# One written-out order replaced by another: a retention layer and a channel mix on one core

## The chip, the core and the metric

The kernel runs on one core of a Trainium2 chip. Five engines work on it side by side, each with an instruction queue that it takes in order: TensorE (PE; its weight loads are PEld), VectorE (DVE), ScalarE (ACT), GpSimd (POOL) and SyncE (SP). The metric is the device time of one execution in microseconds (us). Beside it the profile of one execution gives the span, from its first to its last instruction.

## What is computed

Inputs are q, k and v (4 sequences, 8 heads, 768 tokens, 64 numbers) and the weights of a channel mix. First comes a recurrence over the tokens, per sequence and head, then the mix over the 512 joined numbers of a token:

```python
state = gamma * state + outer(k[t], v[t]);  x[t] = scale * q[t] @ state
xk = mu_k * x + (1 - mu_k) * x_prev;        xr = mu_r * x + (1 - mu_r) * x_prev
h = maximum(xk @ w_k, 0);                   out = sigmoid(xr @ w_r) * (h * h @ w_v)
```

`x_prev` is x one token earlier. `w_k` is 512x1024, `w_v` 1024x512, `w_r` 512x512.

## The kernel before, in words

**Blocks.** The 4x768 tokens are cut into 12 blocks of 256 tokens, numbered 0 to 11, three to a sequence. The recurrence is done a block at a time in matrix form: scores inside the block, a carried state, and the two added up. Blocks 3 and 4, 6 and 7, 9 and 10 share their mix inputs and key matmuls; the others are done alone.

**Pieces and their order.** No scheduler orders the work. The string `ORDER` (from line 24) holds 637 words, and a loop at the end of the kernel goes through it and issues one piece for each. A word is a code, numbers (block first), after `@` the PSUM banks (there are 8, called 0 to 7), and after `~` the engine: v VectorE, a ScalarE, p GpSimd, s SyncE. A word without `~` is TensorE's. The words of one engine, read from left to right, are that engine's queue. So a word's place sets what it stands behind, and its bank sets which earlier result must have been read before it may start.

**The codes**, with the lines under which the profile books them:

- Loads `lq`, `lk`, `lv` (L230, L235) of q, k, v of a block, `wk`, `wr`, `wv` (L735, L738, L742) of weights. From block 2 on, `lk` and `lv` are two DMAs each. The tiles of q, k and v are rings of four.
- TensorE, small tiles: `Tq`, `Tk` transposes (L272, L278); `S` scores (L318, L331, L339); `C` the block's own state (L366, L384, L395); `I`, `J` what the carried state gives (L441); `Y` what the block itself gives (L462, L478, L489).
- TensorE, full 128x128 tiles: `K` the keys xk @ w_k (L572 for the paired blocks, four matmuls of 512 columns; L582 for the others, eight of 256); `R` the gate xr @ w_r (L612, four of 512); `V` the values (L624; a word is four matmuls of 512, so a row block of 128 tokens takes the words V.n.t.0 and V.n.t.1); `Vc` the last row block cut in two halves of columns (L642, eight of 256).
- ScalarE: `Eq`, `Ek` copy the transposes out of PSUM (L241); `t` weights x for block 0 (L542); `Qa` the relu (L591), `Qb` the square (L599, L603), `s` the sigmoid (L618).
- VectorE: `vs` scales v by its decay (L253); `M` masks the scores (L347, L354); `U` adds the carried state (L419); `D` writes x out of PSUM (L507, L514); `dx` the token difference (L529); `X.n.w.j` one quarter j of a block's mix input, w = 0 for xk and 1 for xr (L552 for block 0, else L558); `O` sigmoid times value (L630), `Oc` for the halves (L649). Some `vs`, `U` and `G` words are given to another engine.
- `G` decays the carried state: four instructions on ScalarE (L424), or one on VectorE (L428).
- SyncE: `st` stores a row block of `O` (L637), 128 tokens by 512; `sc` stores a half (L657).
- `z` are matmuls of zeros before and between the first pieces (L703, L710).

**Rings.** A tile is written again only when its readers are done. The results of `O` lie in a ring of four, so `O.n.t` needs the store of block n-2, same t, to have landed. The sigmoids lie in a ring of four as well, the relu outputs too, and `vs` in a ring of three.

The loop that turns words into instructions sets the banks like this:

```python
for word in ORDER.split():
    word, _, at = word.partition("@")
    word, _, eng = word.partition("~")
...
        BANK[key] = [int(x) for x in at]
    CODES[code](ENG.get(eng), *args)
```

Of the kernel before, what the change touches and what calls it, by code (L numbers as in the profile page):

```python
# [29 lines left out]
t.0.0.3~a t.0.0.2~a t.0.0.1~a lv.2~p z.2@4 S.1.1@23 M.1.1~v C.1@01 U.1.0~v z.2@4 I.1@23 S.1.0@67  # L30
X.0.0.1~v t.0.1.2~a X.0.0.2~v Tk.2@0 t.0.1.3~a t.0.0.0~a M.1.0~v X.0.0.0~v z.2@4 Y.1 t.0.1.1~a
X.0.0.3~v Ek.2~a K.0.0@0 K.0.1@6 lq.4~p U.1.1~v G.1~a wr~p lk.4~p D.1~v dx.1~v X.1.0.2~v X.1.0.0~v
K.0.2@1 Qa.0.0~a Qb.0.0~a Qa.0.2~a lq.3~p X.1.0.1~v X.1.0.3~v X.1.1.0~v Qa.0.1~a K.0.3@0 Qa.0.3~a
# [2 lines left out]
Qb.0.2~a Tq.4@01 Eq.4~a Y.2 Qa.1.3~a Qb.1.1~a X.0.1.3~v X.1.1.3~v R.1.1@4 Tk.4@01 Ek.4~a J.2 R.1.0@6
Qa.1.2~a s.1.0~a X.0.1.2~v X.0.1.1~v X.0.1.0~v R.0.1@5 s.0.1~a s.1.1~a R.0.0@7 s.0.0~a S.4.1@01
Qb.1.0~a D.2~v dx.2~v X.2.0.2~v X.2.0.0~v S.4.0@23 Tq.3@4 Eq.3~a X.2.0.1~v wv.1~p X.2.0.3~v Tk.3@7
lq.5~p Ek.3~a K.2.2@5 Qa.2.2~a K.2.3@4 M.4.1~v M.4.0~v Qa.2.3~a Qb.2.3~a lk.6~p S.3.1@67 M.3.1~v
# [7 lines left out]
lq.7~p K.3.7@6 Qa.3.3~a Qa.3.7~a lv.6~p lq.8~p vs.6~v M.5.1~v V.2.0.1 st.0.1~s I.5@67 O.2.0~v
st.2.0~s C.6@23 U.6.0~a U.6.1~v U.6.2~v K.3.6@1 Qa.3.6~a lk.9~p X.3.1.3~v Y.5 Tq.7@45 Eq.7~a U.6.3~v
X.3.1.2~v I.6@01 J.5 X.3.1.0~v D.5~v X.3.1.1~v Qb.3.3~a G.6~a V.2.1.0@2 K.3.1@3 V.2.1.1 O.2.1~v
Qb.3.7~a Qa.3.1~a Qb.3.1~a dx.5~v K.3.4@4 K.3.5@5 Qa.3.5~a X.5.0.0~v X.5.0.3~v R.3.1@2 s.3.1~a  # L50
lv.7~p Qa.3.4~a X.5.0.1~v Qb.3.4~a R.3.0@5 R.4.0@2 s.3.0~a s.4.0~a Qb.3.0~a X.5.0.2~v vs.7~v K.5.2@4
S.7@67 st.1.1~s M.7~v Qb.3.5~a Y.6 Qb.3.6~a lv.10~p C.7@23 U.7.0~v X.5.1.1~v Qa.5.2~a K.5.0@5
R.4.1@6 Qa.5.0~a D.6~v s.4.1~a V.4.0.0@4 V.4.0.1 V.3.1.0@5 U.7.1~v Qb.5.0~a X.5.1.3~v U.7.2~v I.7@01
X.5.1.2~v U.7.3~v Tq.8@67 Eq.8~a X.5.1.0~v O.4.0~v lv.8~p vs.8~v Qb.5.2~a lq.10~p lk.8~p Tk.8@23
Ek.8~a V.3.1.1 V.3.0.0@4 C.8@67 O.3.1~v st.2.1~s st.3.1~s Y.7 dx.6~v D.7~v Tq.10@23 V.3.0.1 Eq.10~a
G.7~a dx.7~v X.6.0.2~v V.4.1.0@5 R.5.1@2 s.5.1~a K.5.3@0 Qa.5.3~a R.5.0@2 U.8.0~v O.3.0~v V.4.1.1
lv.9~p lk.10~p lq.9~p Tk.10@01 s.5.0~a U.8.1~v X.6.0.1~v Ek.10~a X.6.0.0~v Tk.9@23 Ek.9~a K.5.1@7
Qa.5.1~a X.6.0.3~v K.6.0@4 lq.11~p Qb.5.1~a Qa.6.0~a U.8.2~v I.8@01 vs.9~v S.8@23 M.8~v O.4.1~v
st.4.1~s K.6.4@7 Qa.6.4~a vs.10~v X.6.1.2~v K.6.2@6 C.9@23 Qa.6.2~a Qb.6.2~a U.9.0~a Y.8 U.9.1~v
D.8~v U.9.2~v U.9.3~v X.6.1.3~v Qb.5.3~a Tq.9@45 V.5.1.0@6 V.5.1.1 O.5.1~v Eq.9~a lk.11~p K.6.3@7  # L60
Qa.6.3~a K.6.7@4 Qa.6.7~a V.5.0.0@7 C.10@45 Qb.6.0~a X.6.1.0~v S.9@23 M.9~v G.9~a Qb.6.3~a Tq.11@01
Eq.11~a V.5.0.1 dx.8~v X.6.1.1~v st.4.0~s K.6.1@6 Qb.6.7~a Qa.6.1~a Qb.6.1~a X.8.0.3~v X.8.0.0~v
U.10.0~v U.10.1~v K.6.5@2 Qa.6.5~a st.3.0~s lv.11~s K.6.6@0 Qa.6.6~a Qb.6.6~a R.6.0@6 s.6.0~a
O.5.0~v U.10.2~v U.10.3~v R.7.0@2 s.7.0~a R.6.1@7 s.6.1~a I.9@45 X.8.0.2~v S.10@23 Tk.11@01 Ek.11~a
# [6 lines left out]
Qa.9.2~a Qb.9.2~a X.11.0.3~v K.9.5@7 K.9.3@3 K.9.0@2 Qa.9.0~a Qb.9.6~a V.8.0.0@0 V.8.0.1 Qb.9.0~a
Qa.9.5~a Qb.9.5~a Qa.9.3~a O.7.1~v st.7.1~s X.9.1.2~v X.11.0.1~v O.6.0~v K.9.7@1 R.8.1@7 s.8.1~a
K.9.1@5 R.8.0@7 X.9.1.3~v X.11.0.2~v st.6.1~s O.8.1~v R.9.1@4 R.9.0@6 K.11.0@3 K.11.3@2 s.8.0~a
Qa.9.1~a Qb.9.1~a Qb.9.3~a V.10.0.0@5 V.9.0.0@7 Qa.11.0~a Qb.11.0~a Qa.11.3~a s.9.0~a K.9.4@6
R.10.0@2 Qa.9.7~a X.11.1.3~v st.6.0~s K.11.1@1 Qa.11.1~a Qa.9.4~a K.11.2@3 Qb.9.7~a Qb.9.4~a
Qa.11.2~a X.11.1.2~v O.8.0~v st.7.0~s st.8.1~s st.8.0~s V.9.1.0@1 V.10.1.0@6 s.10.0~a V.9.1.1
# [723 lines left out]
```

## Time and profile before

| | before |
|---|---|
| time, median of 3 runs | 153.07 us (153.02 to 153.23) |
| time of the profiled execution | 153.06 us |
| its span | 151.3 us |
| busy: PE, DVE, ACT, POOL | 143.5, 127.5, 103.4, 55.3 us |
| mean granted TensorE clock | 1.000 |
| DMA: bytes, of which GpSimd's queue | 22.16 MB, 14.42 MB |

The profile's page gives the busy time of each engine, the same in 40 slices of the span, and groups of instructions with the mean length of one. Other views list the instructions of one engine in order of time, count busy time in chosen stretches, and tell for the instructions of one line how long they took and how long their DMAs took to land. A row of the timeline names start, length, engine, line, operation and count; in brackets stands the idle time ahead of it and what ended it. Lengths of neighbours overlap a little, because an engine starts the next instruction before the last one has drained; what a queue advances by is the distance of starts.

### The profile page before, as it was taken

The numbers are of one execution on the slowest core, as the hardware profiler recorded it, in microseconds if no ns is written. First come the engines' busy times: TensorE is split into PE (matmuls) and PEld (weight loads), VectorE is DVE, ScalarE is ACT, GpSimd is POOL, SyncE is SP. The second block draws the span as 40 slices with busy tenths as digits, with TensorE's granted clock in tenths as the row PEclk, the third lists the DMA queues.
The fourth block names the chain that finished last, engine by engine and source line by source line (L and its number), as shares of the span: only waits on it lengthen the run. The fifth ranks groups of instructions, "written<-read, shape, count | busy, mean of one in ns | idle before, by whom it ended". The sixth has DMA issues, their size and how long they took to land.

```text
span 151.3 us, 5540 instructions
## 1 busy us (share of the span) xinstructions
PE 143.5 (95%) x2426; PEld 82.9 (55%) x2426; DVE 127.5 (84%) x212; ACT 103.4 (68%) x195; POOL 55.3 (37%) x65
## 2 busy tenths in 40 slices
PE   7878799999999999999999999999999999999991
...
PEclk9999999999999999999999999999999999999999
DMA  5999999999999999999999019311000005500433
GB/s 126 235 230 194 208 228 195 167 247 215 196 166 203 233 260 119 269 289 197 230 172 122 6 45 281 100 41 39 0 4 0 4 0 215 201 0 0 153 129 139
DMA packets 45624, 22.16 MB, mean 146 GB/s; under 512 B 37400, under 2 KB 41248, under 8 KB 45600
## 3 DMA queue, kind: packets, MB, share of 16 engines
q0 software_dynamic: 38704, 14.42, 74.5%
...
q8 instruction: 19, 0.31, 0.8%
q10 hardware_dynamic: 304, 0.18, 0.6%
...
## 4 chain that ended last, share of the span: by engine, by line
PE 86%; ACT 3%; DVE 3%; POOL 2%; DMA 2%; issue 1%; SPq 0%; DVEq 0%
PE ps L624 27%; PE ps L612 14%; PE ps L572 14%; PE ps L582 13%; PE ps L278 3%; PE ps L441 2%; DMA k2s<-in_k_dram 2%; PE ps L272 2%; DVE a L354 2%; PE ps L478 1%; ACT qT L241 1%; POOL vs L253 1%; PE ps L366 1%; PE ps L462 1%; PE ps L642 1%; POOL k L230 1%
## 5 line engine op out<-in xcount | busy, mean ns | idle before, releaser
L624 PE MATMUL ps<-wv,k2s 128*128 128x512 f16 x184 | 44.1, 380 | 0.0
L591 ACT ACTIVATE kr<-ps 128x512 f32<-128x512 f32 x48 | 27.8, 593 | 12.6 <-PE ps L582 6.6
L624 PEld LDWEIGHTS <-k2s 128*128 128x128 f16 x184 | 17.1, 98 | 18.9 <-ACT k2s L603 0.4
L630 DVE SCALAR_TENSOR_TENSOR os<-ps,rs 128x512 f32<-128x512 f32 x23 | 15.7, 684 | 11.9 <-ACT rs L618 9.4
L612 PE MATMUL ps<-wr,xr 128*128 128x512 f16 x96 | 23.5, 379 | 0.0
L582 PE MATMUL ps<-xk,wk 128*128 128x256 f16 x192 | 23.2, 273 | 0.0
L572 PE MATMUL ps<-xk,wk 128*128 128x512 f16 x96 | 23.0, 379 | 0.0
L618 ACT ACTIVATE rs<-ps 128x512 f32<-128x512 f32 x24 | 13.6, 597 | 12.9 <-PE ps L612 12.1
L230 POOL DMA_DIRECT2D k<-in_k_dram x20 | 17.7, 902 | 10.1 <-PE ps L384 6.8
L582 PEld LDWEIGHTS <-wk 128*128 128x128 f16 x192 | 18.1, 98 | 3.7
L241 ACT COPY qT<-ps 128x1024 f16<-128x1024 f16 (+1 forms) x13 | 12.3, 946 | 9.2 <-PE ps L278 7.8
L558 DVE SCALAR_TENSOR_TENSOR xr<-dx,mu,xT 128x256 f16<-128x256 f32 (+1 forms) x32 | 17.9, 577 | 0.1
L230 POOL DMA_DIRECT2D v<-in_v_dram x18 | 16.0, 911 | 3.9 <-DVE a L354 2.2
L558 DVE SCALAR_TENSOR_TENSOR xk<-dx,mu,xT 128x256 f16<-128x256 f32 (+1 forms) x32 | 17.0, 579 | 0.2
L354 DVE TENSOR_TENSOR a<-ps,c_sb 128x1024 f16<-128x1024 f32 (+1 forms) x14 | 14.6, 1066 | 0.7 <-PE ps L339 0.4
L603 ACT ACTIVATE k2s<-kr 128x512 f16<-128x512 f32 x24 | 14.8, 631 | 0.3
L612 PEld LDWEIGHTS <-xr 128*128 128x128 f16 x96 | 9.1, 98 | 10.7 <-issue 0.5
L572 PEld LDWEIGHTS <-wk 128*128 128x128 f16 x96 | 9.1, 98 | 10.5
L599 ACT ACTIVATE k2s<-kr 128x512 f16<-128x512 f32 x24 | 14.5, 627 | 0.3
L529 DVE TENSOR_TENSOR dx<-xT 128x1024 f32<-128x1024 f32 x11 | 13.4, 1222 | 0.2
L241 ACT COPY kT<-ps 128x1024 f16<-128x1024 f16 (+1 forms) x13 | 12.2, 944 | 1.9 <-PE ps L272 1.4
L253 DVE TENSOR_TENSOR vs<-v,csm_sb 128x1024 f16<-128x1024 f32 x10 | 12.2, 1217 | 0.0
...
## 6 DMA issues: line engine op xcount, KB each, us to landing
...
```

The source lines that it names most:

```text
L230: e.dma_start(out=dst[:, :, i * D : i * D + D], in_=src[:, i * P : i * P + P].rearrange("h p d -> p h d"),)
L241: e.copy(out=out, in_=in_)
L354: nc.vector.tensor_tensor(out=a_full(n)[:, i, :, j0:j1], in0=pairs(banks("S", n, i, j0))[:, :, j0:j1], in1=(below if wide(n) else causal[: ...
L558: nc.vector.scalar_tensor_tensor(out=XM[w](k)[:, j, t0:t1], in0=DX(k)[:, j, t0:t1], scalar=mu[:, w * NCO + j : w * NCO + j + 1], in1=x[:, ...
L572: nc.tensor.matmul(banks("K", n, g), lhsT=wk16[:, co, g * P : g * P + P], rhs=XM[0](k)[:, co, :], start=(co == 0), stop=(co == NCO - 1),)
L582: nc.tensor.matmul(pz[:, i, :], lhsT=wk16[:, co, fo * P : fo * P + P], rhs=XM[0](k)[:, co, m * TM + t0 : m * TM + t1], start=(i == 0 and c ...
L591: nc.scalar.activation(out=kr, in_=banks("K", n, g, *u), func=AF.Relu)
L599: nc.scalar.activation(out=k2s[:, n % 3 : n % 3 + 2, g, :], in_=kr, func=AF.Square,)
L603: nc.scalar.activation(out=K2(n)[:, w * g : w * g + w, t0:t1], in_=kr.rearrange("p a t -> p (a t)").rearrange("p (i t) -> p i t", i=w), fu ...
L612: nc.tensor.matmul(banks("R", n, tb), lhsT=XM[1](k)[:, co, t : t + P], rhs=wr16[:, co, :], start=(co == 0), stop=(co == NCO - 1),)
L624: nc.tensor.matmul(banks("V", n, tb), lhsT=K2(n)[:, fo, tb * P : tb * P + P], rhs=wv16[:, fo, :], start=(fo == 0), stop=(fo == NFO - 1),)
L630: nc.vector.scalar_tensor_tensor(out=OS(2 * n + tb), in0=banks("V", n, tb), scalar=1.0 / (KSC * KSC), in1=RS(2 * n + tb), op0=ALU.mult, op ...
```

## The change

All words from the scores of block 1 on are put in another order; the 59 words ahead of them stay. Both orders hold the same 637 words when engine and bank are left aside. Beside the order, 118 words get other banks, and three words another engine: `vs.3` goes from GpSimd to VectorE, `G.9` and `G.10` from ScalarE to VectorE. Functions, tile shapes, rings and transfers are the same. Of the diff, which replaces 51 lines of `ORDER` by 51, the lines that the text below speaks of:

```diff
-lk.3~p vs.2~v Tq.2@1 X.1.1.2~v K.1.3@6 K.1.0@0 C.2@7 U.2.0~v lv.3~p Eq.2~a S.2.1@23 M.2.1~v S.2.0@45
-M.2.0~v Qb.0.3~a lv.4~p K.1.1@1 X.1.1.1~v Qa.1.0~a t.0.1.0~a K.1.2@7 I.2@23 Qb.0.1~a Qa.1.1~a wv.0~p
...
-S.3.0@01 vs.3~p C.3@23 U.3.0~a Qb.2.2~a K.2.1@4 Qa.2.1~a K.2.0@2 Qa.2.0~a I.3@45 lq.6~p vs.4~v
-C.4@67 U.3.1~v X.2.1.1~v V.0.1.0@3 M.3.0~v V.1.0.0@2 G.3~a U.4.0~v I.4@01 X.2.1.3~v U.4.1~v J.3
...
-O.1.0~v Tq.6@01 Eq.6~a Tk.6@45 Ek.6~a st.0.0~s lk.7~p st.1.0~s V.1.1.0@3 V.1.1.1 O.1.1~v s.2.0~a
...
-dx.10~v X.9.0.3~v X.9.0.0~v Y.11 Qb.8.0~a X.9.0.2~v R.7.1@6 s.7.1~a X.9.0.1~v V.7.0.0@7 V.7.0.1
...
-V.10.0.1 s.9.1~a O.9.1~v st.9.1~s Qb.11.2~a Qb.11.3~a O.10.0~v st.10.0~s R.10.1@4 V.9.0.1 s.10.1~a
-O.9.0~v R.11.1@4 V.10.1.1 Qb.11.1~a V.11.0.0@7 R.11.0@5 s.11.0~a st.9.0~s Vc.11.1.1@1 s.11.1~a
-O.10.1~v st.10.1~s Oc.11.1.1~v V.11.0.1 O.11.0~v st.11.0~s sc.11.1.1~a Vc.11.1.0@4 Oc.11.1.0~v
-sc.11.1.0~s
+K.1.1@3 Eq.2~a K.1.3@0 X.1.1.0~v vs.2~v C.2@1 X.1.1.2~v S.2.0@67 S.2.1@45 K.1.2@2 Qa.1.3~a Qb.1.3~a
...
+vs.3~v S.3.0@67 Ek.4~a S.4.1@01 M.3.0~v Qb.0.2~a Qa.2.3~a C.3@45 U.3.0~a U.3.1~v K.2.1@2 Qa.2.0~a
+Qb.2.0~a lv.4~p vs.4~v Qa.2.1~a K.2.2@6 Qa.2.2~a wv.0~p wv.1~p I.3@45 Y.3 Qb.2.1~a M.4.1~v C.4@23
+S.4.0@67 lq.6~p V.1.0.0@0 M.4.0~v G.3~a U.4.0~v X.2.1.2~v Qb.2.2~a V.0.1.0@1 U.4.1~v I.4@67
...
+V.2.1.0@6 lk.8~p V.2.1.1 st.0.1~s O.2.1~v Qb.3.2~a dx.5~v X.5.0.3~v Tk.8@01 C.7@45 G.6~a U.7.0~v
+X.5.0.0~v lq.10~p I.6@23 st.2.1~s lv.8~p R.4.1@7 U.7.1~v X.5.0.2~v st.1.0~s Ek.8~a R.3.0@6 Qb.3.7~a
+V.3.1.0@0 V.3.1.1 U.7.2~v s.4.1~a s.3.0~a Tq.8@67 U.7.3~v st.1.1~s Eq.8~a Y.6 I.7@45 X.5.0.1~v
+lk.9~p K.5.1@1 Qa.5.1~a Qb.5.1~a lv.9~p D.6~v dx.6~v K.5.3@6 Qa.5.3~a Qb.5.3~a O.3.1~v st.3.1~s
+V.3.0.0@1 lk.10~p X.5.1.2~v Tq.10@23 Y.7 Eq.10~a vs.8~v Tk.10@67 D.7~v dx.7~v K.5.2@0 Qa.5.2~a
+lq.9~p Ek.10~a G.7~a V.3.0.1 V.4.0.0@0 lq.11~p V.4.0.1 O.4.0~v X.6.0.1~v Tq.9@67 X.6.0.2~v X.6.0.0~v
+X.6.0.3~v C.8@45 Qb.5.2~a S.8@23 V.4.1.0@0 V.4.1.1 Eq.9~a O.3.0~v K.5.0@6 K.6.3@7 Qa.5.0~a Qb.5.0~a
...
+s.8.0~a V.6.1.1 dx.10~v X.9.0.2~v X.9.0.0~v Y.11 V.7.0.0@3 V.7.0.1 R.8.1@0 V.8.1.0@1 Qb.8.3~a
+Qb.8.2~a V.8.1.1 X.9.0.1~v st.5.0~s O.7.0~v O.6.1~v X.9.0.3~v st.6.1~s V.8.0.0@4 X.9.1.1~v K.9.7@5
...
+V.10.1.1 st.8.1~s s.9.0~a s.10.1~a O.10.1~v V.10.0.0@2 V.10.0.1 O.10.0~v Qb.11.1~a V.9.1.0@5 O.9.0~v
+s.9.1~a V.9.1.1 O.9.1~v Vc.11.1.1@3 R.11.1@2 s.11.1~a st.9.1~s st.10.0~s st.10.1~s Oc.11.1.1~v
+sc.11.1.1~a R.11.0@5 s.11.0~a V.11.0.0@2 V.11.0.1 st.9.0~s O.11.0~v st.11.0~s Vc.11.1.0@3
+Oc.11.1.0~v sc.11.1.0~s
```

SyncE's queue before is, from its first store: st.0.0, 1.0, 0.1, 2.0, 1.1, 2.1, 3.1, 4.1, 4.0, 3.0, lv.11, st.5.1, 5.0, 7.1, 6.1, 6.0, 7.0, 8.1, 8.0, 9.1, 10.0, 9.0, 10.1, 11.0, sc.11.1.0. After it is: st.0.0, 2.0, 0.1, 2.1, 1.0, 1.1, 3.1, lv.11, st.3.0, 4.0, 5.1, 4.1, 6.0, 5.0, 6.1, 7.0, 8.0, 7.1, 8.1, 9.1, 10.0, 10.1, 9.0, 11.0, sc.11.1.0. GpSimd's queue after takes lk.3 and lq.3 ahead of wr and lq.4, and has 20 loads of blocks 5 to 11 in another order.

More of the change, by code (lines that the diff above doesn't have):

```diff
@@ L29 @@
 wk.1~p G.0~a z.2@6 Tq.1@6 Eq.1~a vs.1~p lq.2~p Tk.1@7 Ek.1~a M.0.0.0.2~v M.0.1.2.4~v Y.0 D.0~v
[L30 to L33, printed above, removed]
-lk.3~p vs.2~v Tq.2@1 X.1.1.2~v K.1.3@6 K.1.0@0 C.2@7 U.2.0~v lv.3~p Eq.2~a S.2.1@23 M.2.1~v S.2.0@45
@@ L35 @@
-M.2.0~v Qb.0.3~a lv.4~p K.1.1@1 X.1.1.1~v Qa.1.0~a t.0.1.0~a K.1.2@7 I.2@23 Qb.0.1~a Qa.1.1~a wv.0~p
[L36 to L39, printed above, removed]
-S.3.0@01 vs.3~p C.3@23 U.3.0~a Qb.2.2~a K.2.1@4 Qa.2.1~a K.2.0@2 Qa.2.0~a I.3@45 lq.6~p vs.4~v
@@ L47 @@
[L47 to L64, printed above, removed]
@@ L65 @@
-X.8.0.1~v K.8.1@7 Qb.6.5~a Qa.8.1~a Qb.8.1~a vs.11~v st.5.1~s K.8.0@6 C.11@01 M.10~v Qb.6.4~a
-X.8.1.0~v X.8.1.2~v Y.9 D.9~v G.10~a U.11.0~v st.5.0~s U.11.1~v U.11.2~v Qa.8.0~a I.10@23 V.6.1.0@7
-V.6.1.1 O.6.1~v V.6.0.0@4 V.6.0.1 I.11@01 S.11@67 M.11~v dx.9~v V.7.1.0@5 V.7.1.1 Y.10 D.10~v
-dx.10~v X.9.0.3~v X.9.0.0~v Y.11 Qb.8.0~a X.9.0.2~v R.7.1@6 s.7.1~a X.9.0.1~v V.7.0.0@7 V.7.0.1
-K.8.3@6 O.7.0~v X.9.1.0~v D.11~v X.8.1.1~v Qa.8.3~a Qb.8.3~a K.8.2@2 Qa.8.2~a Qb.8.2~a X.8.1.3~v
-dx.11~v X.11.1.0~v X.11.1.1~v X.9.1.1~v V.8.1.0@6 K.9.2@3 X.11.0.0~v K.9.6@7 Qa.9.6~a V.8.1.1
@@ L71 @@
[L71 to L76, printed above, removed]
@@ L77 @@
-V.10.0.1 s.9.1~a O.9.1~v st.9.1~s Qb.11.2~a Qb.11.3~a O.10.0~v st.10.0~s R.10.1@4 V.9.0.1 s.10.1~a
-O.9.0~v R.11.1@4 V.10.1.1 Qb.11.1~a V.11.0.0@7 R.11.0@5 s.11.0~a st.9.0~s Vc.11.1.1@1 s.11.1~a
-O.10.1~v st.10.1~s Oc.11.1.1~v V.11.0.1 O.11.0~v st.11.0~s sc.11.1.1~a Vc.11.1.0@4 Oc.11.1.0~v
-sc.11.1.0~s
+t.0.0.3~a t.0.0.2~a t.0.0.1~a lv.2~p t.0.1.0~a t.0.1.3~a t.0.0.0~a t.0.1.1~a z.2@4 S.1.1@23 M.1.1~v
+lk.3~p C.1@01 U.1.0~v z.2@4 I.1@23 X.0.0.3~v X.0.0.1~v S.1.0@67 M.1.0~v Tk.2@0 Ek.2~a X.0.0.0~v
@@ new lines @@
+z.2@4 Y.1 X.0.0.2~v U.1.1~v G.1~a lq.3~p K.0.0@0 Qa.0.0~a t.0.1.2~a D.1~v dx.1~v X.1.0.1~v X.1.0.0~v
+K.0.1@1 X.1.0.2~v Qa.0.1~a K.0.2@2 Qa.0.2~a K.0.3@0 Qa.0.3~a Qb.0.0~a Qb.0.3~a Tq.2@2 X.1.0.3~v
+K.1.1@3 Eq.2~a K.1.3@0 X.1.1.0~v vs.2~v C.2@1 X.1.1.2~v S.2.0@67 S.2.1@45 K.1.2@2 Qa.1.3~a Qb.1.3~a
+X.0.1.0~v Qa.1.1~a Qb.1.1~a U.2.0~v I.2@01 Qa.1.2~a K.1.0@3 Qa.1.0~a M.2.0~v M.2.1~v Tq.3@6 Eq.3~a
+Qb.0.1~a Y.2 X.0.1.2~v X.0.1.1~v X.1.1.3~v X.0.1.3~v Tk.3@3 Ek.3~a J.2 wr~p R.0.0@4 s.0.0~a D.2~v
+X.1.1.1~v lq.4~p R.0.1@6 s.0.1~a R.1.1@3 s.1.1~a Qb.1.0~a dx.2~v X.2.0.3~v X.2.0.0~v X.2.0.1~v
@@ new lines @@
+X.2.0.2~v S.3.1@67 M.3.1~v Tq.4@45 Eq.4~a lk.4~p Tk.4@01 R.1.0@3 s.1.0~a K.2.3@2 lv.3~p K.2.0@3
+vs.3~v S.3.0@67 Ek.4~a S.4.1@01 M.3.0~v Qb.0.2~a Qa.2.3~a C.3@45 U.3.0~a U.3.1~v K.2.1@2 Qa.2.0~a
+Qb.2.0~a lv.4~p vs.4~v Qa.2.1~a K.2.2@6 Qa.2.2~a wv.0~p wv.1~p I.3@45 Y.3 Qb.2.1~a M.4.1~v C.4@23
+S.4.0@67 lq.6~p V.1.0.0@0 M.4.0~v G.3~a U.4.0~v X.2.1.2~v Qb.2.2~a V.0.1.0@1 U.4.1~v I.4@67
+X.2.1.0~v J.3 D.3~v V.0.0.0@2 X.2.1.3~v V.0.0.1 Y.4 Tq.6@45 G.4~a Qb.2.3~a Qb.1.2~a lq.5~p dx.3~v
+J.4 D.4~v O.0.0~v V.0.1.1 Eq.6~a V.1.0.1 O.1.0~v O.0.1~v X.2.1.1~v dx.4~v X.3.0.1~v V.1.1.0@6
@@ new lines @@
+V.1.1.1 O.1.1~v X.3.1.1~v X.3.0.3~v Tq.5@01 Eq.5~a lk.6~p st.0.0~s lq.7~p Tk.6@23 Ek.6~a R.2.0@7
+V.2.0.0@4 s.2.0~a R.2.1@5 s.2.1~a X.3.0.0~v lk.5~p Tk.5@67 Ek.5~a lv.5~p Tq.7@23 X.3.0.2~v S.6@01
+V.2.0.1 O.2.0~v st.2.0~s vs.5~v K.3.5@6 Qa.3.5~a M.6~v Eq.7~a K.3.6@7 K.3.0@6 Qa.3.0~a S.5.0@23
+M.5.0~v S.5.1@45 C.5@0 Qa.3.6~a K.3.1@1 U.5.0~v Qb.3.5~a X.3.1.0~v Qa.3.1~a K.3.2@2 Qa.3.2~a
+Qb.3.0~a lq.8~p lv.7~p vs.7~v K.3.3@1 Qa.3.3~a I.5@23 lk.7~p Tk.7@67 K.3.7@0 K.3.4@1 Qb.3.1~a
+M.5.1~v lv.6~p Y.5 Ek.7~a S.7@67 X.3.1.2~v vs.6~v J.5 Qa.3.4~a Qb.3.4~a Qa.3.7~a Qb.3.3~a C.6@45
```

22 lines of the change are left out of this document (18 added, 4 removed).

## The prediction

> **What bounds the kernel now.** I read the page first, then busy time by stretches, then TensorE's instructions in order of time.
>
> ```profile
> span 151.3 us, 5540 instructions
> ...
> PE 143.5 (95%) x2426; PEld 82.9 (55%) x2426; DVE 127.5 (84%) x212; ACT 103.4 (68%) x195; POOL 55.3 (37%) x65
> ...
> PE   7878799999999999999999999999999999999991
> ...
> PEclk9999999999999999999999999999999999999999
> DMA  5999999999999999999999019311000005500433
> ```
> ```profile
> 20.00:30.00 10.00, 10.00 (x161) 7.95 (x159) 9.85 (x16) 8.84 (x18) 7.13 (x9) 1.00 1.67 197
> ...
> 120.00:130.00 10.00, 10.00 (x49) 4.56 (x48) 9.82 (x19) 6.88 (x14) 0.00 (x0) 1.00 0.31 117
> 130.00:140.00 10.00, 10.00 (x64) 6.01 (x62) 0.59 (x2) 7.04 (x15) 0.00 (x0) 1.00 0.11 41
> ```
> ```profile
> 19.47 3.67 PE L582 MATMUL ps<-xk,wk 128*128 128x256 f16 x32
> ...
> 37.76 0.44 PE L384 MATMUL ps<-vs,k 128*64 128x64 f16 x16 [0.26 <-POOL vs L253]
> ```
>
> The columns of the stretches are the length, then busy us and count of PE, PEld, DVE, ACT and POOL, the granted clock, the DMA share and GB/s. From about 20 us on TensorE is never idle but for 0.26 us at 37.76, and its clock is full. VectorE is as good as full too, until 130. The DMA engines are full from 4 to about 80 us. The profiled execution took 153.06 us, so 1.76 lie outside the span; the median of the runs is 153.07.
>
> Busy need not mean full speed, so I look at the distance of starts near the end:
>
> ```profile
> 145.32 1.04 PE L642 MATMUL ps<-wv,k2s 128*128 128x256 f16 x8
> ...
> 146.19 1.03 PE L624 MATMUL ps<-wv,k2s 128*128 128x512 f16 x4
> ...
> 147.05 1.04 PE L642 MATMUL ps<-wv,k2s 128*128 128x256 f16 x8
> ...
> 148.13 0.42 DVE L649 SCALAR_TENSOR_TENSOR os<-ps,rs 128x256 f32<-128x256 f32 x1 [0.18 <-PE ps L642]
> 148.58 0.33 SPq L657 DMA_DIRECT2D out_dram<-os  x1
> ```
>
> A word of full tiles advances the queue by 0.865 us (145.32, 146.19, 147.05) and lasts 1.04 with its drain. The last one, Vc.11.1.0, starts at T = 147.05; its result is stored at T + 1.53. The span ends 2.7 after that store is issued.
>
> **The change, part by part.**
>
> *TensorE's own work: 0.* The words are the same. What an order can change is how often full and small tiles alternate, and from K.0.0 on small tiles stand between full ones in 25 runs in the old order and in 25 in the new. With each word's distance to the next read from the trace by the kinds of the two words (187 words, from that at 19.47 to that at 147.05), the new order adds up to 0.1 more than the old. I take 0, bounds 0.2 to either side for the pairs that the old order doesn't have.
>
> *Before K.0.0: 0.* Each queue holds the same number of words of each kind ahead of it; only the quarters of X and t change places.
>
> *The hand-over at blocks 3 and 4: 0.1.* These rows give the prices of VectorE, and ScalarE's relu:
>
> ```profile
> L591 ACT ACTIVATE kr<-ps 128x512 f32<-128x512 f32 x48 | 27.8, 593 | 12.6 <-PE ps L582 6.6 <-PE ps L572 6.0
> ...
> L529 DVE TENSOR_TENSOR dx<-xT 128x1024 f32<-128x1024 f32 x11 | 13.4, 1222 | 0.2
> L253 DVE TENSOR_TENSOR vs<-v,csm_sb 128x1024 f16<-128x1024 f32 x10 | 12.2, 1217 | 0.0
> ...
> L558 DVE SCALAR_TENSOR_TENSOR xr<-dx,mu,xT 128x256 f16<-128x256 f32 x20 | 9.1, 477 | 0.0
> ...
> L419 DVE TENSOR_TENSOR tg<-ps,tg 128x256 f16<-128x256 f32 x20 | 8.4, 418 | 0.5 <-ACT tg L424 0.2
> ...
> L507 DVE TENSOR_TENSOR xT<-ps,gy_sb 128x512 f32<-128x512 f32 x12 | 8.3, 690 | 0.7
> ...
> L253 POOL TENSOR_TENSOR vs<-v,csm_sb 128x1024 f16<-128x1024 f32 x2 | 3.8, 1906 | 3.8 <-DMA v<-in_v_dram 3.8
> ```
>
> The old idle 0.26 is C.3 waiting for vs.3, 1.91 on GpSimd. Now vs.3 takes 1.22 on VectorE. Adding the words of both queues from D.1 on, vs.3 ends about 0.15 after TensorE is ready for C.3. A little later V.1.0.0 takes bank 0, which M.4.1 must have read; M.4.1 stands behind vs.3, M.3.0 and vs.4 and ends about 0.3 too late. Against the old wait this is +0.1; bounds -0.3 (neither wait) and +0.6 (both, and the old one not saved).
>
> *VectorE's 1.8 us more: 0 by itself.* vs.3 adds 1.14 net of the 0.08 overlap, G.9 and G.10 0.34 each at the price of a U of the same shape. VectorE is full, so the question is where TensorE would notice. The tightest place is the first K.9, which needs the four X.9.0. The new queue has 4.4 us more in front of the last of them (vs.3, G.9, G.10, X.8.1.1, X.8.1.3, O.6.0, O.7.1, O.7.0), and TensorE has four more full words in front of that K (R.8.0, R.8.1, V.8.1.1, V.8.0.0): 3.46. The quarter that comes last is now j = 3, read by the fourth of the four matmuls, and was j = 1, read by the second: two matmuls of 0.216 later, 0.43. One idle gap of VectorE closes:
>
> ```profile
> DVE a L347 <- PE ps L318: 0.9, 2, 0.7
> ```
>
> That is 4.4 against 3.46 + 0.43 + 0.7 = 4.6: just in time. Likewise ScalarE's hand-overs: where a bank is taken again two full words later, 1.73 stand against 1.04 + 0.60 (the relu or sigmoid) and two signals, some 0.05 to spare; there are 13 such places now and 9 before. I take 0, bounds 0 and +1.0 (13 places at 0.08).
>
> *A burst of three stores in front of O.3.1: +0.45.* SyncE's queue now has st.2.1, st.1.0 and st.1.1 in a row. All three start when O.2.1 is done, and O.3.1, whose tile st.1.1 empties, may not write before st.1.1 has landed. Stores early, and after 120 us:
>
> ```profile
> DMA to landing us min/median/max: 4.4/6.2/7.2
> ```
> ```profile
> DMA to landing us min/median/max: 2.0/2.0/2.3
> ```
>
> The loads of blocks 9 to 11 are still running at that time (69 us), so the first row holds. Issues follow each other by 0.4, so st.1.1 lands 0.8 + 6.2 to 0.8 + 7.2 = 7.0 to 8.0 after O.2.1, more if three at once slow each other. Between O.2.1 and O.3.1 VectorE has dx.5, dx.6 (1.14 each net), four X.5.0 (0.40 each), four U.7 (0.34), D.6 (1.3) and some 0.6 of waits for TensorE's Y.6 and for its own results: 7.1. The wait is -0.1 to 0.9, or up to 2.2 with a slowed burst; I take 0.7. TensorE notices it at K.5.2, whose bank 0 O.3.1 empties (0.5 to spare), and at V.4.1.0, whose bank O.4.0 empties, behind vs.8, D.7 and dx.7: some 0.25 less than the wait reaches it. So +0.45, bounds 0 and 2.0. The Trainium skill, in DMA: Bandwidth & Descriptors, section Queues, rings and completion order, says that each DMA engine takes turns between the queues that have work, a packet at a time, so a store isn't queued behind the loads. By that alone stores would take little more beside loads than after them, and this term would be 0, the sum about 153.65; the rows, 6.2 against 2.0, speak against it here.
>
> *The end: +0.5.* In the old order the stores of blocks 9 and 10 go out one by one. In the new one SyncE has st.9.1 ahead of st.10.0, st.10.1 and st.9.0, and O.9.1 comes only behind V.9.1.1, six full words before the last: that word ends at T - 5.19 + 1.03, O.9.1 at T - 3.4. All four stores go out from there, 0.38 apart, the last at T - 2.3. O.11.0 needs st.9.0 landed; it is ready itself at T + 0.2, when V.11.0.1 has ended. With 2.0 the store lands in time; with each store 0.65 behind the one ahead (the 2.3 is a store issued 0.4 behind another: 0.4 + 0.3) it lands at T + 0.7, later with Oc.11.1.1's store beside it: I take T + 0.9. O.11.0 (0.69) then pushes Oc.11.1.0 from T + 1.08 to T + 1.55: +0.5. Bounds 0 and 1.3. The Trainium skill, in DMA: Bandwidth & Descriptors, section Anatomy of one DMA, has a fixed 2.0 us plus the bytes at 436 GB/s, 0.6 us for 256 KB, for GpSimd's DMAs; one behind the other, four such stores would land at T + 1.0, an estimate, and the term would be about 0.6.
>
> Sum: 153.06 + 0.1 + 0.45 + 0.5 = **154.1 us**. Its own range, with one of the two store terms at an end, is 153.4 to 155.0.
>
> **The rivals.**
>
> *Both store waits are hidden* (0.15): st.1.1 lands within 7.1 us of its burst and st.9.0 by T + 0.2. Then 0.1 is left: 153.1. For it: stores took as little as 4.4 beside loads. Against: two of the six took 6.8 and more.
>
> *The new order has fewer small waits* (0.18, the faster side). The old order loses 0.26 at C.3, and 0.14 here, where two words of 0.865 from 64.51 would end at 66.24:
>
> ```profile
> 64.51 1.89 PE L572 MATMUL ps<-xk,wk 128*128 128x512 f16 x8
> 66.38 2.75 PE L612 MATMUL ps<-wr,xr 128*128 128x512 f16 x12
> ```
>
> With some smaller ones, 0.2 by my estimate, 0.6 could go: 153.06 - 0.6 = 152.5. It decides at V.1.0.0: if M.4.1 has ended when V.1.0.0's turn comes, and the stores land in time. Against: the sum of VectorE's words puts M.4.1 0.3 late.
>
> *VectorE's extra work isn't absorbed* (0.25). The balance at K.9 is 0.2 us from tipping, and a wait of VectorE before it, such as that at O.3.1, is carried along. With 1.0 lost there, the store wait at 1.5 and the end at 0.5 the time is 153.06 + 0.1 + 0.95 + 1.25 + 0.5 = 155.9.
>
> That the change doesn't do what it says is no rival: the words are the same, but for three engines.
>
> **How the numbers follow.** Forecast 0.42, hidden stores 0.15, fewer waits 0.18, not absorbed 0.25. A measurement of this kernel can tell about 0.2% (0.3 us) from no change. Slower: 0.42 + 0.25 = 0.67; same 0.15; faster 0.18. The range from 152.7 to 156.1 leaves out about half of the fast case and a third of the slow one, 0.17 in all. Where the slow cases alone hold, it is 153.4 to 156.1.
>
> **What the new profile would show.** If the steps are right: TensorE starts its first K at 19.5 as before; a short wait of C.3 or V.1.0.0 near 37 to 41 us; VectorE idle ahead of a result (L630) near 76 us, released by a store's DMA; no idle time of TensorE at the first K.9, near 121 us; and at the end O.11.0 (L630) waiting for a store, not for TensorE. VectorE's last X (L558) should end near 130 as before. It is wrong if TensorE waits for ScalarE at many places, if a load (k, q or v) comes late, as those of blocks 3 and 4 might, with wr now behind lk.3 and lq.3, or if the time falls below 152.7.

## The result, and the profile after

| | before | after |
|---|---|---|
| time, median | 153.16 us, 6 runs (153.02 to 153.55) | 159.70 us, 6 runs (158.96 to 160.81) |
| profiled execution, its span | 153.06, 151.3 | 160.68, 158.9 |
| mean granted TensorE clock, runs | 1.00 | 0.985 to 0.996 |

The ratio is 1.042 (95% interval 1.037 to 1.047): slower by 6.5 us, outside the range that was given. Three of the six executions after had a mean clock under 0.99 and took 160.2 to 160.8, the profiled one among them; the other three took 159.0 to 159.2.

The page after, for the lines shown of before:

```profile
span 158.9 us, 5535 instructions
...
PE   7879759999999999999939999999999999999990
...
PEclk9999999999999999999995999999999999999999
DMA  5999999999999999989998030003030030310082
```

TensorE has two dents that it did not have, in slices 6 and 21 (a slice is 4.0 us), and its clock one, in slice 22. The stretch with the second, in columns as in the prediction's stretches:

```profile
80.00:90.00 10.00, 7.27 (x114) 3.65 (x114) 6.66 (x9) 4.77 (x9) 0.00 (x0) 0.83 0.57 99
```

**First dent.** Timeline of the kernel after, around it:

```profile
21.04 0.58 ACT L591 ACTIVATE kr<-ps 128x512 f32<-128x512 f32 x1
21.52 0.50 ACT L542 ACTIVATE dx<-xT,nu 128x256 f32<-128x256 f32 x1
...
22.04 1.23 DVE L514 TENSOR_TENSOR xT<-ps,gy_sb 128x1024 f32<-128x1024 f32 x1 [2.01 <-ACT dx L542]
23.32 1.91 PE L582 MATMUL ps<-xk,wk 128*128 128x256 f16 x16 [1.75 <-DVE xT L514]
```

`D.1` (L514) waits 2.01 for a `t` (L542) on ScalarE, which stands behind the relu `Qa.0.0` (L591) of a key word that TensorE has only just done. `D.1` is what empties bank 2, and `K.0.2` waits 1.75 for that. Before, `D.1` did not wait:

```profile
19.77 1.22 DVE L514 TENSOR_TENSOR xT<-ps,gy_sb 128x1024 f32<-128x1024 f32 x1
```

**Second dent.** Around it:

```profile
70.92 0.69 DVE L630 SCALAR_TENSOR_TENSOR os<-ps,rs 128x512 f32<-128x512 f32 x1
71.64 11.39 SPq L637 DMA_DIRECT2D out_dram<-os  x4
...
77.58 1.22 DVE L529 TENSOR_TENSOR dx<-xT 128x1024 f32<-128x1024 f32 x1
...
81.98 0.69 DVE L630 SCALAR_TENSOR_TENSOR os<-ps,rs 128x512 f32<-128x512 f32 x1 [3.18 <-DMA out_dram<-os]
82.73 1.03 PE L582 MATMUL ps<-xk,wk 128*128 128x256 f16 x8 [2.75 <-DVE os L630]
83.60 4.44 PE L624 MATMUL ps<-wv,k2s 128*128 128x512 f16 x12
```

`O.2.1` ends at 71.61, the three stores go out from 71.64, and `O.3.1` waits 3.18 for the third. `K.5.2` then waits 2.75 for its bank. The 12 matmuls behind it are three words, which at 0.865 each and 0.17 of drain take 2.77; here they take 4.44. The trace has the granted clock at 0.5 for 3.41 us from 83.85 on: 4.44 - 2.77 = 1.67 us more. Before, `O.3.1` did not wait:

```profile
77.58 0.68 DVE L630 SCALAR_TENSOR_TENSOR os<-ps,rs 128x512 f32<-128x512 f32 x1
```

**The end.**

```profile
150.58 5.37 SPq L637 DMA_DIRECT2D out_dram<-os  x5
...
152.79 0.42 DVE L649 SCALAR_TENSOR_TENSOR os<-ps,rs 128x256 f32<-128x256 f32 x1 [2.24 <-DMA out_dram<-os]
...
153.67 0.60 ACT L618 ACTIVATE rs<-ps 128x512 f32<-128x512 f32 x1 [1.54 <-DVE os L649]
...
153.93 1.04 PE L642 MATMUL ps<-wv,k2s 128*128 128x256 f16 x8
154.89 0.69 DVE L630 SCALAR_TENSOR_TENSOR os<-ps,rs 128x512 f32<-128x512 f32 x1 [1.67 <-DMA out_dram<-os]
155.50 0.41 DVE L649 SCALAR_TENSOR_TENSOR os<-ps,rs 128x256 f32<-128x256 f32 x1
156.04 0.38 SPq L657 DMA_DIRECT2D out_dram<-os  x1
```

The last word starts at T = 153.93 and the last store goes out at T + 2.11; before it was T + 1.53. `O.11.0` waits for a store, as forecast, and so does `Oc.11.1.1`, behind which ScalarE's last sigmoid stands.

TensorE's two waits, the half clock and the later last store (2.11 - 1.53) add up to 1.75 + 2.75 + 1.67 + 0.58 = 6.75 of the 7.6 by which the profiled spans differ.

### The profile page after: what moved, and what is told of

Its sections match the earlier page's. It is cut to its first block, busy times and chain, and to the rows that moved or that the text cites. A ratio compares the mean times of both kernels' runs of the same rounds, so it can differ in the third digit from the quotient of the medians.

```text
span 158.9 us, 5535 instructions
## 1 busy us (share of the span) xinstructions
PE 146.0 (92%) x2426; PEld 83.4 (52%) x2426; DVE 129.7 (82%) x215; ACT 101.1 (64%) x187; POOL 53.4 (34%) x64
## 4 chain that ended last, share of the span: by engine, by line
PE 57%; DVE 18%; DMA 15%; ACT 3%; issue 3%; SPq 1%; DVEq 0%; POOLq 0%
PE ps L624 22%; PE ps L572 12%; PE ps L612 8%; DMA out_dram<-os 8%; PE ps L582 7%; DVE a L354 5%; DMA v<-in_v_dram 4%; DMA k<-in_k_dram 3%; DVE vs L253 3%; DVE os L630 2%; DVE xk L558 2%; DVE xT L514 2%; DVE dx L529 1%; PE ps L278 1%; PE ps L441 1%
## 5 line engine op out<-in xcount | busy, mean ns | idle before, releaser
L624 PE MATMUL ps<-wv,k2s 128*128 128x512 f16 x184 | 44.9, 390 | 0.1
L591 ACT ACTIVATE kr<-ps 128x512 f32<-128x512 f32 x48 | 27.9, 593 | 25.7 <-PE ps L572 13.3
L624 PEld LDWEIGHTS <-k2s 128*128 128x128 f16 x184 | 17.9, 100 | 21.1 <-issue 2.4
L572 PE MATMUL ps<-xk,wk 128*128 128x512 f16 x96 | 21.9, 379 | 0.0
L603 ACT ACTIVATE k2s<-kr 128x512 f16<-128x512 f32 x24 | 14.7, 626 | 0.3
L253 DVE TENSOR_TENSOR vs<-v,csm_sb 128x1024 f16<-128x1024 f32 x11 | 13.3, 1216 | 0.1
```

The costliest lines, as they stand in the source:

```text
L253: e.tensor_tensor(out=VS(n), in0=V32(n).rearrange("p h (i d) -> p i h d", i=2), in1=gks[:, int(half(n) or wide(n)), :, :, None].to_broadca ...
L572: nc.tensor.matmul(banks("K", n, g), lhsT=wk16[:, co, g * P : g * P + P], rhs=XM[0](k)[:, co, :], start=(co == 0), stop=(co == NCO - 1),)
L591: nc.scalar.activation(out=kr, in_=banks("K", n, g, *u), func=AF.Relu)
L624: nc.tensor.matmul(banks("V", n, tb), lhsT=K2(n)[:, fo, tb * P : tb * P + P], rhs=wv16[:, fo, :], start=(fo == 0), stop=(fo == NFO - 1),)
```

## The experiments

The runs of one group were on one chip, beside runs of the kernel before, whose median was 153.25 to 153.36 in all four groups. The kernel after was run once more (under 3): 158.92, 7 runs. All its 13 runs have a median of 159.2, and gains are told from that. The runs are called by the first part of their labels, e1 to e10 and a2. The diffs show words of `ORDER`; "..." leaves words out.

**1. D.1's wait.** The theory: the wait is for a read that touches nothing that `D.1` writes. `D.1` writes the columns of block 1 in each of the four parts j of xT; `t.0.1.2` reads those of block 0, one to the left, in part 2. None is in common, but as addresses the read lies between the first and the last element written. If `t.0.1.2` comes first in the string, `D.1` is made to wait for it, so the theory. In the old order the late quarter was `t.0.1.0`, behind `D.1` in the string.

```diff
-Qa.0.0~a t.0.1.2~a D.1~v dx.1~v
+Qa.0.0~a D.1~v t.0.1.2~a dx.1~v
```

> The kernel after, with one word moved: t.0.1.2 stands behind D.1 in the order, so the queues of VectorE and ScalarE are what they were, and only who must wait for whom between the two is turned round. Theory: D.1's 2.0 us of waiting is a wait for a read (t.0.1.2) that touches none of the elements D.1 writes; then it goes, TensorE's 1.75 us ahead of K.0.2 go too, and the time falls by 1.5 to 2.1 us against the kernel after, to about 157.7. D.1 (L514) shows no idle time ahead of it that ScalarE ended. Rival: the gap comes from ScalarE's queue (the relu Qa.0.0 ahead of t.0.1.2); then K.0.2 goes on waiting and the time stays within 0.3 us of the kernel after.

Measured: 158.14 us (157.72 to 158.91). The timeline:

```profile
19.65 3.67 PE L582 MATMUL ps<-xk,wk 128*128 128x256 f16 x32
19.95 1.22 DVE L514 TENSOR_TENSOR xT<-ps,gy_sb 128x1024 f32<-128x1024 f32 x1
21.04 0.58 ACT L591 ACTIVATE kr<-ps 128x512 f32<-128x512 f32 x1
21.52 0.50 ACT L542 ACTIVATE dx<-xT,nu 128x256 f32<-128x256 f32 x1
```

ScalarE does the same at the same times, `D.1` runs 2.09 earlier, and TensorE goes through 32 matmuls without a stop. So the wait comes from the order in the string, and the rival (ScalarE's queue) falls. What is not shown is why the order counts for slices that share no element: the addresses that lie between each other would do, and so would a rule that goes by the whole tile; no run tells these two apart. The gain, 1.0, is less than the 1.75 that went, and less than was expected. In this profile another wait is there:

```profile
56.60 0.69 DVE L630 SCALAR_TENSOR_TENSOR os<-ps,rs 128x512 f32<-128x512 f32 x1 [1.12 <-DMA out_dram<-os]
...
59.62 0.32 PE L384 MATMUL ps<-vs,k 128*64 128x64 f16 x8 [1.10 <-DVE a L347]
```

VectorE waits 1.12 at `O.2.0` for a store, which TensorE feels at `C.5`. The first profile of the kernel after has no such wait, but its second one (a2, an execution of 162.4 us) has, with the 1.75 at `K.0.2` still in place:

```profile
62.60 0.32 PE L384 MATMUL ps<-vs,k 128*64 128x64 f16 x8 [1.60 <-DVE a L347]
```

So this wait comes in some executions with either order of the two words, and how much of the missing gain is due to it stays open.

The converse is the old order with this one wait:

```diff
-t.0.1.2~a ... D.1~v ... Qa.0.0~a ... t.0.1.0~a
+t.0.1.0~a ... Qa.0.0~a t.0.1.2~a D.1~v
```

> The kernel before, with the quarters t.0.1.0 and t.0.1.2 changed for each other and t.0.1.2, behind the relu Qa.0.0, put ahead of D.1 in the order, as the kernel after has them; nothing else. Theory (this place alone costs D.1 a wait of 2.0 us, for a read that touches none of its elements): D.1 (L514) waits 1.9 to 2.1 us for ScalarE's L542, TensorE is idle 1.7 us ahead of K.0.2, and the time is 1.4 to 2.1 us above the kernel before. Rival (in the old order later slack takes it up): the wait is there and the time is less than 0.5 us above before.

Measured: 157.17 us (156.35 to 157.80), 3.8 above before.

```profile
21.78 1.22 DVE L514 TENSOR_TENSOR xT<-ps,gy_sb 128x1024 f32<-128x1024 f32 x1 [2.01 <-ACT dx L542]
25.23 3.72 PE L582 MATMUL ps<-xk,wk 128*128 128x256 f16 x16 [1.62 <-ACT k2s L603]
...
39.37 2.37 PE L582 MATMUL ps<-xk,wk 128*128 128x256 f16 x16 [0.80 <-DVE xk L558]
```

The same wait of 2.01, but it costs more than the 1.4 to 2.1 that were expected, and elsewhere: `K.0.2`, which has bank 1 here, does not wait; TensorE loses 1.62 at `K.1.3`, then 0.80, where VectorE is still behind, and in two of the four executions (clock 0.988, 157.8 against 156.4 and 156.6) 1.3 more. In the profiled one of these the clock is at half for 3.41 us from 26.02 on. The bracket names a square (L603), but before, `K.1.3` starts at 23.64, ahead of that square (24.66). What is later is `X.1.0`, which `K.1.3` reads and which stands behind `D.1` and `dx.1`: it starts at 24.30 against 22.28.

**2. The burst of stores.** SyncE's queue, stores alone:

```diff
-st.0.0 st.2.0 st.0.1 st.2.1 st.1.0 st.1.1 st.3.1
+st.0.0 st.1.0 st.2.0 st.1.1 st.0.1 st.2.1 st.3.1
```

> The kernel after, with two stores issued earlier in SyncE's queue: st.1.0 ahead of st.2.0, st.1.1 ahead of st.0.1, so that st.2.1 goes out alone at 70 us. Theory (the burst costs the wait of 3.2 us at O.3.1, TensorE's 2.75 us ahead of K.5.2, and the half clock behind it about 1.7 us more): O.3.1 waits under 0.5 us, the granted clock is 1.0 throughout, and the time falls by 3.5 to 4.5 us, to about 155.5. Rival (the half clock has another cause and comes anyway): the wait goes, the clock still falls to 0.5 near 80 us, and the time falls by 2.3 to 2.8.

Measured: 156.55 us (156.03 to 157.10), a gain of 2.6, and no execution with a mean clock under 0.99. The gain lies in the rival's range, but what the rival says would come, half a clock near 80 us, does not. Timeline, then the landing of the stores: the six from 48 to 77 us, `st.2.1` alone, and last the three in a row in the kernel after:

```profile
79.20 0.68 DVE L630 SCALAR_TENSOR_TENSOR os<-ps,rs 128x512 f32<-128x512 f32 x1
...
80.72 1.05 PE L582 MATMUL ps<-xk,wk 128*128 128x256 f16 x8
```
```profile
DMA to landing us min/median/max: 6.2/6.9/8.2
```
```profile
DMA to landing us min/median/max: 6.2/6.2/6.2
```
```profile
DMA to landing us min/median/max: 8.6/9.0/9.4
```

`O.3.1` no longer waits, nor does `K.5.2`. `st.2.1`, issued at 72.11 with no other store beside it, took 6.2; first of three, issued at 71.64 in the kernel after, it took 8.6, and the two behind it 9.0 and 9.4. The loads that GpSimd issued from 70 to 75 us took 6.2 to 8.0 here and 7.0 to 9.6 there. So about 6 us are there without the burst, and the burst adds 2.4 to 3.2. (The 8.2 is the last of three stores that now go out in a row at 58 us.) The gain stays 0.9 below what was expected; two new stops of TensorE, 0.52 and 0.16, with nothing to wait for, are taken up under 5.

**3. The half clock.** One matmul of zeros cuts the idle time in two, with no work sped up.

```diff
-Tk.10@67 ... K.5.2@0
+Tk.10@67 ... z.4@2 K.5.2@0
```

> The kernel after, with one matmul of zeros more (512 columns in f32, into bank 2, which ScalarE empties at 80.8) ahead of K.5.2, so that TensorE's idle time of 2.75 us there is cut in two of about 0.8 and 1.0. Nothing else is sped up. Theory (the idle time of 2.75 us is what the clock falls for): K.5.2 starts as late as in the kernel after, but the granted clock stays 1.0 behind it in every execution, the mean clock of all runs is 0.995 or more, and the slower ones of the kernel after (clock 0.985 to 0.989, span 158.7 to 159.0) don't come: median about 158.9. Rival (the half clock comes from something else, as the load of the engines there): some executions still show a mean clock under 0.99, and the median stays at 159.7.

```profile
81.43 1.13 PE L703 MATMUL ps<-zero 128*128 128x512 f32 x2 [0.86 <-ACT qT L241]
83.02 1.03 PE L582 MATMUL ps<-xk,wk 128*128 128x256 f16 x8 [0.47 <-DVE os L630]
```

Measured: 159.20 us (158.60 to 160.47), clocks 0.994 to 1.000. `K.5.2` starts as late as before, and no execution is under 0.99. Four are few, so it was run again beside the kernel after.

> The same kernel as e6_zeros_in_gap, for more executions. In the kernels with TensorE's idle time of 2.7 us whole ahead of K.5.2 (after, e1, e5), 6 of 14 executions had a mean clock under 0.99; in e6_zeros_in_gap none of 4. Theory (the idle time in one piece is what the clock falls for): again none of the executions here is under 0.99. Rival (the four were chance): about 3 of 6 to 7 are.

> The kernel after as it is, on the same chip beside e6b, for the share of executions with a mean clock under 0.99. Theory: about half of them, and these are 1.2 to 1.7 us longer than the others; the median is 0.3 to 0.8 us above that of e6b. Rival (the clock is a matter of the chip and the hour, not of the kernel): the same share as in e6b.

Measured: 158.70 us (158.58 to 159.17), none of five under 0.99. The kernel after: 158.92 us (158.55 to 162.37), two of seven under 0.99, at 160.0 and 162.4, against 158.6 to 159.8 for the others. Together 8 of 21 executions with the idle time whole (after, a2, e1, e5), and none of 9 with it cut. Were the 8 spread by chance over all 30, none among these 9 would come about once in 29 times. The kernels in which the store's wait at `K.5.2` is gone (e2, e3, e7, e10) had none in 18 either. So the evidence is that the clock falls for the idle time, though not each time: the profiles of e1 and e5 have 2.71 and 2.69 of it and stay at full clock. Where the clock fell is seen in the two profiles of the kernel after alone; of the other executions only the mean is known (half of 3.41 us in a span of 158.9 makes 0.989). The medians of the last two runs differ by 0.2 only, less than expected. The kernel before had two such executions in 36, so this is not its only cause.

**4. The end.**

```diff
-st.9.1~s st.10.0~s st.10.1~s ... st.9.0~s
+O.10.1~v st.10.1~s ... O.10.0~v st.10.0~s ... O.9.0~v st.9.0~s ... O.9.1~v st.9.1~s
```

> The kernel after, with only the last four stores moved: each of st.10.1, st.10.0, st.9.0 right behind its own O, all ahead of st.9.1. Theory (the four stores in a row cost 0.5 to 0.6 us at the end): the time falls by 0.5 to 0.6 us against the kernel after; O.11.0 (the last L630) waits for TensorE, not for a store; the last store goes out 1.5 us after the start of Vc.11.1.0. Rival (the end is set by TensorE's last words whatever the stores do): no change.

Measured: 159.26 us (157.80 to 160.49): no gain that these few runs can tell. The profile is clearer.

```profile
152.80 0.60 ACT L618 ACTIVATE rs<-ps 128x512 f32<-128x512 f32 x1 [1.61 <-DVE os L649]
152.98 1.04 PE L642 MATMUL ps<-wv,k2s 128*128 128x256 f16 x8
153.43 0.69 DVE L630 SCALAR_TENSOR_TENSOR os<-ps,rs 128x512 f32<-128x512 f32 x1 [1.08 <-ACT rs L618]
...
154.57 0.38 SPq L657 DMA_DIRECT2D out_dram<-os  x1
```

The last store goes out at T + 1.59, 0.52 earlier. But `O.11.0` waits for ScalarE's sigmoid now: on ScalarE it stands behind `sc.11.1.1`, which needs `Oc.11.1.1`, which needs `st.9.1`. So one wait is gone and the other is left; the last store goes out 0.06 later than in the kernel before (T + 1.53).

**5. All three, and what was behind them.**

> The kernel after with all three edits: t.0.1.2 behind D.1, two early stores moved forward, the last stores each behind its own O. Theory (these three places and the clock behind the second are the whole loss): 2.0 + 2.75 + 1.7 + 0.6 go, and the time is 152.5 to 153.3, within 0.3% of the kernel before. Rival (some of the loss is the new order's many small waits, or VectorE's 1.8 us more of work): the time stays at 153.6 or above, with idle time of TensorE spread over places other than these.

Measured: 156.09 us (154.38 to 156.62). The theory falls: 2.7 above before are left. That is the rival's time, but not its picture of many small places: the profile (156.62) has one large stop, in the middle of `Tq.10`, and its page this line (packets, MB, share of 16 engines):

```profile
77.00 0.32 PE L278 MATMUL ps<-c_sb,q 64*64 64x64 f16 x16
...
79.17 0.32 PE L278 MATMUL ps<-c_sb,q 64*64 64x64 f16 x16 [1.86 <-issue]
```
```profile
q8 instruction: 19, 0.31, 0.9%
```

"issue" is a stop for which the profile shows no releaser, and the first half of the word has read the same tile already. TensorE's 4852 instructions (2426 weight loads and as many matmuls) over 19 packets are 255 a packet. The theory is that it fetches them in blocks of 256, by DMA. In experiment 2 it stops so at two weight loads that are 384 apart, here at the second of these and at one 128 behind it (in the trace's count, from 1, they are numbers 991, 1375 and 1503; the expectation has them four higher). Each weight load has its matmul, so these places lie 768 and 256 instructions apart. If that is the cause, moving eight instructions ahead of the word must move the stop inside it:

```diff
-V.3.0.0@1 ... Tq.10@23 Y.7 ... Tk.10@67 ... K.5.2@0 ... V.3.0.1
+V.3.0.0@1 ... V.3.0.1 Tq.10@23 Y.7 ... Tk.10@67 ... K.5.2@0
```

> The kernel with all three edits (e3_all_three), and V.3.0.1, four full matmuls with their weight loads, moved from behind Tk.10 to ahead of Tq.10. In e3_all_three TensorE stood 1.86 us still in the middle of Tq.10, behind its 16th matmul of 32, with no semaphore to wait for; its weight loads with such stops are numbers 995 (in e2_stores_apart), 1379 and 1507, 384 and 128 apart, which is a multiple of 256 instructions, and a queue of DMAs of kind instruction moved 19 blocks of 16 KB for 4843 instructions. Theory (TensorE waits for the next block of 256 instructions, fetched by DMA behind the loads): eight instructions more stand ahead of Tq.10, so the stop, if there is one, comes behind its 12th matmul, and it is shorter by up to 0.9 us, since a full word more runs meanwhile. Rival (Tq.10 waits for its data or for bank 3): the stop stays behind the 16th matmul, or at the start of the word.

```profile
77.88 0.29 PE L278 MATMUL ps<-c_sb,q 64*64 64x64 f16 x12
...
79.18 0.35 PE L278 MATMUL ps<-c_sb,q 64*64 64x64 f16 x20 [1.02 <-issue]
...
81.89 1.89 PE L624 MATMUL ps<-wv,k2s 128*128 128x512 f16 x8 [0.68 <-ACT kr L591]
```

Measured: 155.80 us (154.91 to 156.85). The stop comes behind the 12th matmul and ends when it did, at 79.18; it is 0.84 shorter, since the word put ahead of it used the time, and 0.68 of that is lost again at `V.4.0.0`, now close behind `K.5.2`. So the theory holds and the rival falls. The instruction packets in the trace fit: TensorE goes on 1.40 to 1.46 after one has landed (77.75 and 79.17 in e3, 77.73 and 79.18 in e7, 59.85 and 61.25, 78.34 and 79.79 in e2).

So there was little to spare everywhere. In the old order the same block was fetched by 76.39, which by 1.4 allows 77.8, and TensorE reached it at 78.13. The old order takes 7.3 us of work over the block ahead of it (70.80 to 78.13), the new one, with three edits, 4 (73.33 to 77.3, where it stops): more small tiles in a row.

Two full words ahead of `Tq.10` should cover the rest; at the end `s.11.0` goes ahead of `sc.11.1.1`:

```diff
-V.3.0.0@1 ... Tq.10@23 Y.7 ... K.5.2@0 Qa.5.2~a ... V.3.0.1
+V.3.0.0@1 ... V.3.0.1 K.5.2@0 Qa.5.2~a Tq.10@23 Y.7
...
-sc.11.1.1~a R.11.0@5 s.11.0~a
+R.11.0@5 s.11.0~a sc.11.1.1~a
```

> The kernel with all three edits (e3_all_three), with two full words, V.3.0.1 and K.5.2 with its relu Qa.5.2, ahead of Tq.10, and at the end ScalarE's sigmoid s.11.0 ahead of the DMA sc.11.1.1, which waits for a store. Theory (what is left in e3_all_three is mostly the fetch of instructions at Tq.10, 0 to 1.9 us, and 0.3 us at the end; the rest, 0.8, is the new order's small words): TensorE's stop is behind the 4th matmul of Tq.10, at most 0.5 us long, O.11.0 follows V.11.0.1 at once and the last store goes out 1.5 to 1.6 us after the start of Vc.11.1.0; the median is 154.0 to 154.9. Rival (the fetch was no loss of its own, and another wait takes its place): 155.6 or more, with a wait at V.4.0.0 or behind.

```profile
148.60 1.04 PE L642 MATMUL ps<-wv,k2s 128*128 128x256 f16 x8
148.86 0.69 DVE L630 SCALAR_TENSOR_TENSOR os<-ps,rs 128x512 f32<-128x512 f32 x1 [1.08 <-PE ps L624]
...
150.12 0.33 SPq L657 DMA_DIRECT2D out_dram<-os  x1
```

Measured: 154.76 us (154.48 to 156.24). No stop at `Tq.10`, the end at T + 1.52, and `O.11.0` waits for TensorE alone. Single executions overlap with those of e3 (154.38 to 156.62), so the 1.3 between the medians is not clear of noise; the profile is. Two of six executions took 156.2 at full clock; why, stays open. From `K.0.0` to the last word the profile has 128.59 us against 127.58 before: 1.0 more, all of it in runs of small tiles (22.59 against 21.60). `C.6` and `Tq.9`, which hold such block boundaries, make up 0.63 of it, with stops of 0.23 and 0.14 that end 1.22 and 1.52 after a packet has landed; the rest is the balance of many words that differ by 0.1 to 0.4, and what sets those stays open. Another 0.5 of the spans' difference lies ahead of `K.0.0`, which this profile reaches at 20.01; the profiles of the new order reach it between 19.38 and 20.03, always with the same words ahead of it. The kernel before stays the fastest, and nothing found here points to one that beats it.

**6. VectorE's extra work.** The three words back on their old engines, in the kernel with all three edits:

```diff
-vs.3~v ... G.9~v ... G.10~v
+vs.3~p ... G.9~a ... G.10~a
```

> The kernel with all three edits (e3_all_three), with vs.3 on GpSimd and G.9 and G.10 on ScalarE, as in the kernel before. Theory (VectorE's 1.8 us more work is absorbed, as the prediction had it): within 0.5 us of e3_all_three, median 155.6 to 156.6. Rival (it delays TensorE somewhere): over 0.8 us faster than e3_all_three, 155.2 or less.

```profile
35.17 2.05 POOL L253 TENSOR_TENSOR vs<-v,csm_sb 128x1024 f16<-128x1024 f32 x1 [8.66 <-DVE xk L558]
37.18 1.80 POOL L230 DMA_DIRECT2D v<-in_v_dram  x2
...
42.90 1.23 DVE L253 TENSOR_TENSOR vs<-v,csm_sb 128x1024 f16<-128x1024 f32 x1 [3.76 <-DMA v<-in_v_dram]
...
44.18 0.44 PE L384 MATMUL ps<-vs,k 128*64 128x64 f16 x16 [3.39 <-DVE vs L253]
```

Measured: 164.41 us (163.73 to 166.45, which is the profiled one): neither theory nor rival. The new order has `lv.4` behind `vs.3`; on GpSimd `vs.3` holds up that load's issue, to 37.18 against 25.88 in e3. TensorE waits 3.39 at `C.4`, the clock halves behind that, and near 117 it does so again behind an idle time of 2.06. There `G.10`, back on ScalarE, stands ahead of the square `Qb.6.4`, which `V.6.0.0` needs: it waits 1.50 for a `U` of VectorE, and the square starts only at 116.09. The run says nothing on VectorE's load. It shows that the new order, with its queues as they are, is slower with the old engines.

## Why the prediction was wrong, step by step

| step | forecast | measured |
|---|---|---|
| order ahead of `K.0.0`, and the quarters changed | 0 | 0.2 at `K.0.0`, less than profiles of one order differ by; 1.75 at `K.0.2` through `D.1` (e1 wins 1.0, e4 loses 3.8) |
| hand-over at blocks 3 and 4 | 0.1 more than the old wait | two waits of 0.03 and 0.06 in place of the old 0.26: 0.2 less |
| VectorE's 1.8 more | 0 | no idle time at the first `K.9` |
| wait at `O.3.1` | 0.7, of which 0.45 reach TensorE | 3.18, of which 2.75 |
| half clock behind it | not in the sum | 1.7 when it comes |
| the end | 0.5 | 0.58 |
| TensorE's own words | 0, bounds 0.2 | up to 1.0 (e10), with the fetch of instructions in it |

Direction and two of the places were right; the size was not, for three reasons. The second, with the third behind it, is the largest: 2.75 + 1.67 in the profile, against 0.45.

**"Before K.0.0: 0 ... only the quarters of X and t change places."** This step failed. I compared queues word by word and asked who stands behind whom on one engine. I did not ask, for each word that changed places, which writer on another engine has to wait for it. `t.0.1.2` was such a reader of xT, and its new place made the wait even though no element is shared; e1 took it away by moving the word across `D.1` alone. The sum had no term at all for the stretch from `K.0.0` to block 3, where the wait is felt. Nor do the queues hold the same words ahead of `K.0.0`: `U.1.1`, `G.1`, `lk.3` and `lq.3` stand ahead of it in the new string only, though `K.0.0` itself starts only 0.2 later in the profile.

**The store term** had the right mechanism and places, mis-sized. The row of stores in the old order, 4.4 to 7.2, was taken as the length of a store at that time. For one store alone that holds (6.2 in e2); three at once took 8.6 to 9.4. "Up to 2.2 with a slowed burst" was the bound, and 3.2 came. VectorE arrived at 78.80, 7.2 after `O.2.1`, as worked out (7.1).

**The clock** was left out, since the trace of before shows it full throughout. I let an idle time cost what it lasts. In the Trainium skill, TensorE: Matmul & The Clock Gate, section HAM oscillation — how this bites in real kernels, the rule is no idle gaps of TensorE over some 3.4 us. Here the measurements go against that figure: idle times of 2.75 and, in e4, of 1.62 were followed by half clock, in some of the executions. Others were not, such as the 1.75 of the first dent and the 1.86 in e3, so the length alone does not decide. The same page, Part 1: The HAM clock gate, has a free-running window of 3413 ns; the stretches at half clock in the middle of these traces last 3.41, once 6.83, which agrees.

The end came as forecast, with a second chain (`st.9.1`, `Oc.11.1.1`, `sc.11.1.1`, `s.11.0`) that I had not seen and that bound next in e5. That VectorE's work costs nothing has only the missing wait at `K.9` for it; no run isolated it. The rival "not absorbed", 155.9, had the right sign but the wrong place; its sum has 0.95 where its text says 1.0, which changes nothing.
